# A list schedule that also picks the engine, and separate tiles for the first eight heads

## The chip, the cores and the metric

One Trainium2 chip, one of its cores. The metric is the device time of one execution in microseconds. The engines are named as in the profile: PE (TensorE, with its weight loads as PEld), DVE (VectorE), ACT (ScalarE), POOL (GpSimd), SP (SyncE, which here only issues DMAs). [...]

## What is computed

Attention whose queries and keys only meet when their hash buckets agree, for 4 batches of 8 heads (768 positions, head width 64), and behind it a feed-forward layer over 3072 tokens, 512 to 2048 to 512:

```python
q_bits = (np.einsum('bhsd,dk->bhsk', q, proj) > 0)      # six sign bits, k likewise
mask = q_bucket[:, :, :, None] == k_bucket[:, :, None, :]
scores = np.where(mask, scale * q @ k.T, -1e9)
attn = exp(scores - max) / (sum + 1e-9)
x = (attn @ v), heads side by side: 3072 x 512
g = s * relu(x @ w_in) ** 2 + b
out = g @ w_out
```

All inputs are 32-bit floats, except the two feed-forward weights, which arrive as 64-bit floats.

## The kernel before

**Work and staging.** The unit of attention work is a *slot*: 256 query rows of one head of one batch. There are 3 slots in a head, 24 in a batch, 96 in all. A *visit* is one head: its `prep` transposes queries and keys, splits both in a rounded high part and a remainder (`aq`, `bq`, `ks`), hashes them, and moves pieces between partitions with DMAs. `weights` makes the scores of a slot on PE (L436, L437), takes their negated maximum on DVE (L441), the exponential and its sum on ACT (L442), the inverse of the sum in four small DVE operations (L446 to L449), and scales the row on POOL (L454); the result is in one of four `eb` buffers. `values` transposes that on PE (L479), copies the transposed weights from PSUM to SBUF, and multiplies them with `v`.

For the first eight heads (`FULL = 8`, batch 0, slots 0 to 23) that product is made with plain 32-bit operands (L503; each appears as two matmuls in the profile), from copies that ACT makes for two of the three parts of a slot (L489) and DVE for the third (L487, `FD = (2,)`). For the other heads the copy is rounded on ACT (L494), the remainder is made on DVE (L495), and the product is four rounded matmuls (L510, L511). `values` ends with a copy of 64x256 to `xpb` (L526); every second head, both are split into `xsb` on ACT (L532) and DVE (L533) and sent to DRAM.

**Feed-forward.** `decode` loads one of 32 weight blocks (128x512 numbers of 64 bits) and makes a rounded part and a remainder of it: two ACT operations (L274, L275), two on DVE (L276, L277) and one on POOL (L278) join the two words of each number, then the rounded part is made on ACT (L280) and the remainder on POOL (L281). `moe` does one chunk of 256 tokens in eight steps, 96 steps in all: 24 matmuls of 256 columns (L569 to L571), three ACT operations (L575 to L577), two on POOL (L578, L579), and 12 matmuls of 512 columns (L590 to L592). A chunk can begin when it is through all eight heads of its batch, so the first comes behind slot 21.

**What sets the order.** Every operation is a step of `Plan` with an engine, a cost in microseconds that is written beside it, what it reads and writes, and a priority. `order` plays the engines forward with these costs and, on each, takes the ready step of the best priority; the result is each engine's instruction list, and on the chip each engine runs its list strictly in that order. Attention of slot `i` has priority around `10 * i`, decodes come a little behind, the feed-forward fills in where PE has nothing else. `decodes(i)` says how many of the 32 blocks may have been planned by slot `i`.

**Tiles that change type.** The buffers `PH` (the transposed weights) and `VS` (values) first hold plain 32-bit numbers for the first eight heads; `swap` later puts a tile of the rounded type in the same place.

## Time and profile before

| | |
|---|---|
| timed runs | 1095.40, 1088.42, 1095.47 us; median 1095.4 us |
| profiled execution | 1091.88 us, its span 1090.1 us |
| busy share of the span | PE 97%, PEld 86%, ACT 60%, DVE 56%, POOL 46% |
| instructions | 18596 |

How to read it: PE is the engine that is busy almost throughout, so the time is what PE works plus what it waits. A shown matmul lasts until its result is out, while the next one has begun long before; so waits shorter than that tail do not show as idle time, and the distance between two starts says more than the length. The program has four stretches: start-up (to 20 us), the 24 slots of batch 0 with next to no feed-forward to fill in (to 200 us), attention and feed-forward mixed (to about 880 us), and feed-forward alone.

### The profile page before, as it was taken

What the parts mean: (1) busy time and instruction counts of PE and PEld (TensorE: products, weight loads), DVE (VectorE), ACT (ScalarE), POOL (GpSimd) and SP (SyncE); (2) the same over time, 40 slices, a digit from 0 to 9 for tenths busy, and PEclk for the clock granted to TensorE, in tenths of its full rate; (3) what the DMA queues carried; (4) which work ended last, traced back from release to release, by engine and by line L of the source; (5) the groups of instructions that cost most, each with busy time, mean ns of one, the idle gap of its engine ahead of it and who ended that gap; (6) DMA issues with size and microseconds to landing.
All of it is one profiled execution on the core that took longest, in us unless ns stands there. A gap on an engine that the chain in (4) does not pass through costs nothing.

```text
span 1090.1 us, 18596 instructions
## 1 busy us (share of the span) xinstructions
PE 1062.0 (97%) x6948; PEld 942.4 (86%) x6948; DVE 612.9 (56%) x1181; ACT 654.4 (60%) x1265; POOL 502.1 (46%) x482
## 2 busy tenths in 40 slices
PE   7999888999999999999999999999999999999998
PEld 6666565898899999999999999999999998898987
DVE  5568886888666667666666766566667520000000
ACT  3567776888566666665666666656657553333332
POOL 2346776888644443444444443444444433333333
PEclk8999998999999999999999999999999999999999
DMA  3347565645322423332332243232323010101000
GB/s 80 83 134 201 160 189 141 160 118 175 80 55 62 121 74 82 94 92 65 92 104 64 74 112 84 54 115 66 83 54 118 3 56 33 58 1 59 17 23 20
DMA packets 85643, 94.14 MB, mean 86 GB/s; under 512 B 52832, under 2 KB 57952, under 8 KB 85552
## 3 DMA queue, kind: packets, MB, share of 16 engines
q1 hardware_dynamic: 80352, 75.90, 26.0%
q10 hardware_dynamic: 5200, 17.05, 5.1%
q8 instruction: 55, 0.90, 0.3%
q14 instruction: 36, 0.29, 0.1%
HBM read 48.24 MB, written 18.87 MB: 62 GB/s over the span
## 4 chain that ended last, share of the span: by engine, by line
PE 71%; issue 13%; POOL 8%; DVE 5%; ACT 2%; POOLq 0%; DVEq 0%; ACTq 0%
PE bank L479 11%; PE bank L436 6%; PE bank L437 6%; PE bank L503 5%; PE bank L569 5%; PE bank L570 5%; PE bank L571 5%; PE bank L590 5%; PE bank L511 5%; PE bank L591 5%; PE bank L592 5%; PE bank L510 4%; POOL glb L579 4%; POOL rb L578 3%; PE bank L318 2%
## 5 line engine op out<-in xcount | busy, mean ns | idle before, releaser
L454 POOL TENSOR_SCALAR eb<-eb,st 128x768 f32<-128x768 f32 x192 | 191.9, 1008 | 217.9 <-DVE st L449 175.2
L569 PE MATMUL bank<-xc,w 128*128 128x256 f32 x768 | 224.5, 292 | 0.0
L441 DVE TENSOR_REDUCE st<-bank 128x1 f32<-128x768 f32 x192 | 182.8, 954 | 73.9 <-PE bank L437 71.4
L570 PE MATMUL bank<-xc,w 128*128 128x256 f32 x768 | 217.0, 283 | 0.0
L571 PE MATMUL bank<-xc,w 128*128 128x256 f32 x768 | 216.9, 282 | 0.0
L442 ACT ACTIVATE eb<-bank,st 128x768 f32<-128x768 f32 x192 | 173.2, 903 | 43.3 <-DVE st L441 36.1
L494 ACT CAST phr<-bank 128x512 fp32r<-128x512 f32 x216 | 125.2, 583 | 123.1 <-PE bank L479 122.0
L578 POOL TENSOR_SCALAR rb<-rb,misc 128x512 f32<-128x512 f32 x96 | 74.8, 779 | 267.0 <-ACT ghb L577 255.7
L495 DVE TENSOR_TENSOR plb<-bank,phr 128x512 fp32r<-128x512 f32 x216 | 147.1, 686 | 80.2 <-ACT phr L494 77.9
L479 PE MATMUL bank<-ident,eb 128*128 128x128 f32 x1152 | 169.0, 276 | 4.4 <-POOL eb L454 2.9
L590 PE MATMUL bank<-w,ghb 128*128 128x512 f32 x384 | 156.5, 407 | 0.0
L592 PE MATMUL bank<-w,glb 128*128 128x512 f32 x384 | 151.4, 394 | 1.9 <-POOL glb L579 1.9
L591 PE MATMUL bank<-w,ghb 128*128 128x512 f32 x384 | 152.6, 398 | 0.0
L479 PEld LDWEIGHTS bank<-ident,eb 128*128 128x128 f32 x1152 | 135.8, 142 | 17.8 <-POOL eb L454 4.8
L569 PEld LDWEIGHTS bank<-xc,w 128*128 128x128 f32 x768 | 146.0, 190 | 4.3 <-issue 0.4
L570 PEld LDWEIGHTS bank<-xc,w 128*128 128x128 f32 x768 | 146.2, 190 | 3.1
L575 ACT ACTIVATE rb<-bank 128x512 f32<-128x512 f32 x96 | 57.5, 598 | 148.1 <-PE bank L571 145.7
L571 PEld LDWEIGHTS bank<-xc,w 128*128 128x128 f32 x768 | 146.0, 190 | 0.0
L436 PE MATMUL bank<-ks,aq 128*128 128x384 f32 x384 | 139.7, 364 | 3.6 <-ACT eb L442 3.5
L437 PE MATMUL bank<-ks,bq 76*128 76x384 f32 x384 | 131.9, 343 | 1.5 <-DVE bq L395 1.5
L579 POOL TENSOR_TENSOR glb<-rb,ghb 128x512 fp32r<-128x512 f32 x96 | 124.2, 1293 | 6.2
L510 PE MATMUL bank<-phr,vsr 128*128 128x256 f32 x432 | 115.1, 288 | 0.0
(88 smaller groups left out, 1723.3 us busy)
## 6 DMA issues: line engine op xcount, KB each, us to landing
xd<-xsb SPq DMA_DIRECT2D x48, 256.0 KB
xc<-xd SPq DMA_DIRECT2D x48, 256.0 KB
ks<-aq SPq DMA_DIRECT2D x30, 384.0 KB
raw<-in_moe_w_in_dram ACTq DMA_DIRECT2D x16, 512.0 KB
raw<-in_moe_w_out_dram ACTq DMA_DIRECT2D x16, 512.0 KB
nat<-in_q_dram SPq DMA_DIRECT2D x32, 192.0 KB
nat<-in_k_dram SPq DMA_DIRECT2D x32, 192.0 KB
ks<-bq SPq DMA_DIRECT2D x30, 192.0 KB
```

Source lines behind the costliest of these rows:

```text
L436: nc.tensor.matmul(o, aq[:, ts], ks[:, 0, cols], start=True, stop=False)
L437: nc.tensor.matmul(o, bq[0:HR, ts], ks[0:HR, 1, cols], start=False, stop=True)
L441: dve(S, lambda a=a, sc=sc: nc.vector.tensor_reduce(nm[:, a:a + 1], sc, AX.XY, ALU.max, negate=True), bk, [nk[a]], pr, 0.95)
L442: act(S, lambda a=a, sc=sc, e=e: nc.scalar.activation(e.rearrange("p (g n) -> p g n", g=2), sc, AF.Exp, bias=nm[:, a:a + 1], accum_out=z[: ...
L454: pool(S, lambda a=a, e=e: nc.gpsimd.tensor_scalar(e, e, rz[:, a:a + 1], u[:, a:a + 1], ALU.mult, ALU.add), [("st", y, 2)], [ek], pr, 1.01)
L479: nc.tensor.transpose(out=bank[:, tb, o:o + P], in_=eb[:, es[a], kt * P:(kt + 1) * P], identity=ident)
L569: nc.tensor.matmul(hp, w[:, 0, fs], xc[:, 0, :], start=(cc == 0), stop=False)
L570: nc.tensor.matmul(hp, w[:, 1, fs], xc[:, 0, :], start=False, stop=False)
L571: nc.tensor.matmul(hp, w[:, 0, fs], xc[:, 1, :], start=False, stop=(cc == NC_ - 1))
L590: nc.tensor.matmul(o, gh[:, ts], w[:, 0], start=(f == 0), stop=False)
L591: nc.tensor.matmul(o, gh[:, ts], w[:, 1], start=False, stop=False)
L592: nc.tensor.matmul(o, gl[:, ts], w[:, 0], start=False, stop=(f == NF - 1))
```

## The change

Five things change.

1. `Plan.any` takes a step with several *ways*, one for each engine that could do it. `order` lets the engine have it that would end it first by the written costs. Steps with two ways: the copies of transposed weights and of `xpb` (ACT or DVE), the relu (ACT or DVE), the output copies (DVE or ACT), the rounded part of `xsb` and of a decoded weight (ACT or POOL), and two copies of the first two visits (ACT or DVE). These copies all stand in the helper `copy`, L197 of the changed kernel.
2. The remainder of `xsb` moves from DVE to POOL.
3. `PH` and `VS` have the rounded type from the start. The plain values and weights of the first eight heads get tiles of their own, `VF` and `PF` (four of the latter instead of three), in the room of the last four weight blocks; `decode` of those four blocks waits until slot 23 is through with them.
4. The preparation of the first two visits works in halves of 384 columns, transposes queries and keys together (12 transposes instead of 24), and loads into the same layout as all others; the copy of `aq` to both halves of `ks` is two DMAs instead of one with a repeated source.
5. `decodes` starts two slots earlier and at a lower rate (`DSTART`, `FIRST`), four of the written costs change (among them 0.55 instead of 0.70 for the inverse), and the assumed DMA rate rises. `SMALL` and `SPLIT` are switches that keep the old way.

```diff
     def add(self, eng, cost, fn, r=(), w=(), pr=0.0, lag=0.0):
+        self.any([(eng, cost, fn)], r, w, pr, lag)
+
+    def any(self, ways, r=(), w=(), pr=0.0, lag=0.0):
...
+        def best(e, t):
+            found = None
+            for i in open_[e]:
+                if ready[i] > t + LOOK.get(e, 0.0):
+                    continue
+                ways, pr = self.steps[i][:2]
+                if found is not None and found[:2] <= (pr, i):
+                    continue
+                if len(ways) > 1:
+                    mine = max(t, ready[i]) + next(c for x, c, _ in ways if x == e)
+                    if any(max(free.get(x, 0.0), ready[i]) + c < mine - 1e-9 for x, c, _ in ways if x != e):
+                        continue
+                found = (pr, i)
+            return found
...
+    def some(n, fn, r, w, pr, ways):
+
+        cost = {ACT: 0.095 + n / 1050.0, DVE: (n + 64) / 960.0 + 0.05, POOL: 0.15 + n / 760.0}
+        eng = {ACT: nc.scalar, DVE: nc.vector, POOL: nc.gpsimd}
+        plan.any([(e, cost[e], lambda e=e: fn(eng[e])) for e in ways], r, w, pr)
...
-    VS = [wk.tile([P, 2, NT, D], F32, tag=f"vs{x}", name=f"vf{x}") for x in range(2)]
+    VS = [tile_(f"vs{x}", [P, NT, 2, D], F32R) for x in range(2)]
+    VF = [wk.tile([P, NT, D], F32, tag=f"w{ND_ - 1 - x}", name=f"vf{x}") for x in range(2)]
+    PF = [wk.tile([P, 2, 2 * CH], F32, tag=f"w{ND_ - 3 - x}", name=f"pf{x}") for x in range(2)]
+    PF = [z[:, y].rearrange("p (m q) -> p m q", m=2) for z in PF for y in range(2)]
...
-    PH = [wk.tile([P, 2, CH], F32, tag=f"ph{y}", name=f"pf{y}") for y in range(NPH)]
+    PH = [tile_(f"ph{y}", [P, 2, CH], F32R) for y in range(NPH)]
...
-        plan.add(None, 0.0, new, [], rk, pr - 5)
+        held = {ND - 1: [("vf", 0)], ND - 2: [("vf", 1)], ND - 3: [("pf", 0), ("pf", 1)], ND - 4: [("pf", 2), ("pf", 3)]}.get(u, [])
+        plan.add(None, 0.0, new, [], rk + held, pr - 5)
...
-        act(512, lambda: nc.scalar.copy(wt[key][:, 0], g), [gk], [key + (0,)], pr)
+        copy(512, lambda: wt[key][:, 0], lambda: g, [gk], [key + (0,)], pr, (ACT, POOL))
...
-                dma(lambda: ks[0:D], lambda: aq[D:P].rearrange("p (o n) -> p o n", o=1).broadcast_to([D, 2, S]), ...
+                for z in range(2):
+                    dma(lambda z=z: ks[z][0:D], lambda: aq[D:P], AK(x, r=(1,)), [("ks", x, 0, z)], pr, D * S * 4)
...
-        dve(1, inverse, nk + zk, [("st", y, 2)], pr, 0.70)
+            dve(1, inverse, nk + zk, [("st", y, 2), ("st", y, 3)], pr, 0.55)
...
-            if w < FULL:
-                if f in FD:
-                    dve(512, lambda: nc.vector.tensor_copy(ph(), src), [("b", tb)], [("ph", y)], pr, 0.65)
-                else:
-                    act(512, lambda: nc.scalar.copy(ph(), src), [("b", tb)], [("ph", y)], pr)
+            if full:
+                copy(512, lambda: ph, lambda: src, [("b", tb)], [("pf", y)], pr, (ACT, DVE))
                 return y
...
-            act(512, lambda: nc.scalar.copy(ph(), src), [("b", tb)], [("ph", y)], pr)
+            copy(512, lambda: ph, lambda: src, [("b", tb)], [("ph", y)], pr, (ACT, DVE))
...
-            act(CH, lambda: nc.scalar.copy(xsb[:, 0, :], t), xk, [("xs", 0)], pr)
-            dve(CH, lambda: nc.vector.tensor_tensor(xsb[:, 1, :], t, f32(xsb[:, 0, :]), ALU.subtract), ...
+            copy(CH, lambda: xsb[:, 0, :], lambda: t, xk, [("xs", 0)], pr, (ACT, POOL))
+            pool(CH, lambda: nc.gpsimd.tensor_tensor(xsb[:, 1, :], t, f32(xsb[:, 0, :]), ALU.subtract), ...
...
-        return min(ND, int(FIRST * max(0, i - EARLY // 3)) if i < EARLY else 8 + int(RATE * (i - EARLY)))
+        n = int(FIRST * max(0, i - DSTART)) if i < EARLY else int(FIRST * (EARLY - DSTART)) + int(RATE * (i - EARLY))
+        return min(n, ND if i >= H * NCH else ND - 4)
...
-FIRST = 1.2
+FIRST = 0.8
+DSTART = 5
-RATE_DMA = 1.9e5
+RATE_DMA = 2.2e5
```

Places in the instruction lists. `nat`, `aq`, `bq`, `ks` end in 69, 71 and the like for visit 0 (odd heads: 70, 72); `st` holds the maxima and sums, `pf` the transposed weights of the first eight heads, `eb` the exponentials. An `x2` is two instructions of that kind in a row.

DVE at start-up, before: the reductions of slot 0 (L441) come between the two visits' preparations.

```order
L393 TENSOR_SCALAR ks_71<-bank,misc 12x768
L395 TENSOR_SCALAR bq_69<-bank,misc 12x768
L367 TENSOR_TENSOR ks_72<-bank,ks_72 64x768
L441 TENSOR_REDUCE st<-bank 128x1 x2
L375 SCALAR_TENSOR_TENSOR bq_70<-bank,aq_68 64x768
L446 TENSOR_SCALAR st<-st 128x2
L447 TENSOR_SCALAR st<-st 128x2
L448 RECIPROCAL st<-st 128x2
L449 SCALAR_TENSOR_TENSOR st<-st 128x2
L393 TENSOR_SCALAR ks_72<-bank,misc 12x768
L395 TENSOR_SCALAR bq_70<-bank,misc 12x768
```

DVE at start-up, changed (L470 is the reduction):

```order
L427 TENSOR_SCALAR ks_71<-bank,misc 12x384
L429 TENSOR_SCALAR bq_69<-bank,misc 12x384
L406 SCALAR_TENSOR_TENSOR bq_70<-bank,aq_68 64x384
L408 TENSOR_TENSOR ks_72<-bank,ks_72 64x384
L406 SCALAR_TENSOR_TENSOR bq_70<-bank,aq_68 64x384
L408 TENSOR_TENSOR ks_72<-bank,ks_72 64x384
L427 TENSOR_SCALAR ks_72<-bank,misc 12x384
L429 TENSOR_SCALAR bq_70<-bank,misc 12x384
L427 TENSOR_SCALAR ks_72<-bank,misc 12x384
L429 TENSOR_SCALAR bq_70<-bank,misc 12x384
L470 TENSOR_REDUCE st<-bank 128x1 x3
```

All of the second visit's preparation now stands ahead of the first reduction.

DVE in slots 1 to 3, before: one copy of transposed weights (L487) in a slot.

```order
L441 TENSOR_REDUCE st<-bank 128x1 x2
L487 COPY pf_79<-bank 128x512
L441 TENSOR_REDUCE st<-bank 128x1
L446 TENSOR_SCALAR st<-st 128x2
L447 TENSOR_SCALAR st<-st 128x2
L448 RECIPROCAL st<-st 128x2
L449 SCALAR_TENSOR_TENSOR st<-st 128x2
L441 TENSOR_REDUCE st<-bank 128x1
```

The same place, changed (L197 is the copy that may stand on either engine, L487 to L490 the four small operations):

```order
L470 TENSOR_REDUCE st<-bank 128x1 x2
L487 TENSOR_SCALAR st<-st 128x2
L488 TENSOR_SCALAR st<-st 128x2
L489 RECIPROCAL st<-st 128x2
L490 SCALAR_TENSOR_TENSOR st<-st 128x2
L197 COPY pf_78<-bank 128x512
L470 TENSOR_REDUCE st<-bank 128x1
L197 COPY pf_78<-bank 128x512 x2
L487 TENSOR_SCALAR st<-st 128x2
```

DVE has up to two copies in a row here, and the small operations of the next slot stand behind them.

POOL around the first decode, before: scaling of rows (L454) and a decode's two operations (L278, L281), nothing else.

```order
L454 TENSOR_SCALAR eb<-eb,st 128x768 x14
L278 TENSOR_TENSOR osb<-osb,raw_192 128x512
L454 TENSOR_SCALAR eb<-eb,st 128x768 x2
L281 TENSOR_TENSOR w_644<-osb,w_644 128x512
L454 TENSOR_SCALAR eb<-eb,st 128x768 x2
```

POOL around the first decode, changed (L495 scales the rows, L320 and L323 are the decode's, L565 and the two kinds of L197 are new on this engine):

```order
L565 TENSOR_TENSOR xsb<-xpb,xsb 128x256
L495 TENSOR_SCALAR eb<-eb,st 128x768 x2
L320 TENSOR_TENSOR osb<-osb,raw_196 128x512
L197 CAST w_639<-osb 128x512
L197 CAST xsb<-xpb 128x256
L323 TENSOR_TENSOR w_639<-osb,w_639 128x512
L565 TENSOR_TENSOR xsb<-xpb,xsb 128x256
L495 TENSOR_SCALAR eb<-eb,st 128x768 x2
```

Between two scalings there are now up to five other operations.

## The prediction

> **What bounds the kernel now.** I read the page first (shares, slices), then the stretches of the span, then the groups of instructions inside the stretch where PE is not full, then single rows for the true distance of matmuls. The first two lines are PE's share and its forty slices.

> ```profile
> PE 1062.0 (97%) x6948; PEld 942.4 (86%) x6948; DVE 612.9 (56%) x1181; ACT 654.4 (60%) x1265; POOL 502.1 (46%) x482
> PE   7999888999999999999999999999999999999998
> ```

> PE is busy 97% of the span; its slices are under 9 at the start, in slices 4 to 6 and in the last. The stretches say where (columns: PE, weight loads, DVE, ACT, POOL busy, granted clock, DMA share, GB/s):

> ```profile
> 0.00:20.00 20.00, 13.52 (x69) 10.02 (x69) 11.04 (x39) 6.13 (x9) 4.79 (x11) 0.99 0.41 108
> 20.00:200.00 180.00, 167.28 (x887) 116.60 (x887) 134.31 (x253) 126.30 (x258) 102.42 (x90) 0.96 0.54 148
> 200.00:300.00 100.00, 98.35 (x676) 91.00 (x676) 80.05 (x131) 77.65 (x152) 77.14 (x67) 1.00 0.45 126
> 300.00:900.00 600.00, 598.29 (x4165) 560.33 (x4164) 380.44 (x748) 378.82 (x753) 251.02 (x252) 1.00 0.30 79
> 900.00:1080.00 180.00, 179.30 (x1139) 160.88 (x1138) 5.53 (x8) 63.95 (x94) 64.73 (x63) 1.00 0.08 28
> ```

> From 200 us to the end of the table PE idles 4.1 us in 880. What an engine other than PE saves there buys nothing. From 20 to 200 us, the 24 slots of batch 0, PE idles 12.7 us, and its matmuls are too few for the time: 887 in 180 us against 676 in 100 us. Its groups in that stretch, and rows with back-to-back starts:

> ```profile
> L503 PE MATMUL bank<-pf,vf 128*64 128x256 f32 x288 | 73.1, 391 | 5.6 <-ACT pf L489 3.9 <-DVE pf L487 1.5
> L479 PE MATMUL bank<-ident,eb 128*128 128x128 f32 x288 | 42.1, 287 | 3.7 <-POOL eb L454 2.9 <-DVE nat L336 0.8
> L436 PE MATMUL bank<-ks,aq 128*128 128x384 f32 x97 | 38.1, 393 | 2.2 <-ACT eb L442 2.0
> L318 PE MATMUL bank<-ident,nat 128*128 128x128 f32 x48 | 8.5, 287 | 0.0
> L331 PE MATMUL bank<-aq,pjh 128*64 128x384 f32 x15 | 5.8, 385 | 1.2 <-DVE bq L321 1.2
> ...
> 133.76 0.34 PE L436 MATMUL bank<-ks,aq 128*128 128x384 f32 x1
> 133.94 0.34 PE L437 MATMUL bank<-ks,bq 76*128 76x384 f32 x1
> 134.11 1.48 PE L479 MATMUL bank<-ident,eb 128*128 128x128 f32 x12
> 135.52 2.80 PE L503 MATMUL bank<-pf,vf 128*64 128x256 f32 x12
> ```

> Dense, a score matmul takes 0.175 us (133.76 to 134.11 for two), a transpose 0.118 (134.11 to 135.52 for twelve), an L503 at most 0.233 (2.80 for twelve). So the stretch holds 288 x 0.233 + (288 + 48) x 0.118 + 2 x 97 x 0.175 + 3 x 15 x 0.175 = 67 + 40 + 34 + 8 = 149 us of work, with the few feed-forward matmuls at its end about 151. Of the other 29 us some 7 are clock (next rows); some 22 are waits, of which the profile shows 12.7 as idle. These 22 us are what this change can reach.

> ```profile
> 12.00:19.00 7.00, 4.08 (x23) 2.77 (x22) 6.01 (x10) 3.36 (x6) 1.64 (x2) 1.00 0.25 56
> 19.00:26.00 7.00, 7.00 (x26) 5.80 (x26) 4.66 (x5) 2.53 (x6) 1.94 (x2) 0.53 0.00 0
> 165.00:173.00 8.00, 5.90 (x36) 4.50 (x36) 6.03 (x13) 5.75 (x14) 6.75 (x6) 1.00 0.80 201
> 173.00:180.00 7.00, 6.33 (x20) 4.39 (x20) 4.46 (x8) 4.08 (x8) 4.72 (x5) 0.51 0.61 150
> ```

> Twice a stretch in which PE idled two or three microseconds is followed by one of 7 us at half the clock, worth about 3.4 us each. [...] The timed runs lie at 1088.4 and 1095.4, the profiled one at 1091.9: steps of 3.5 us, so I read them (an estimate) as one, three and two such stretches.

> **The change, part by part.** The sum is against the profiled execution, 1091.9 us, 3.5 under the median of 1095.4. DVE, ACT and POOL in the same stretch, 20 to 200 us, with three rows of the whole run at the end (L418, L368, L603):

> ```profile
> L441 DVE TENSOR_REDUCE st<-bank 128x1 f32<-128x768 f32 x49 | 46.2, 952 | 20.8 <-PE bank L437 20.6
> L277 DVE SCALAR_TENSOR_TENSOR osb<-osb,raw 128x512 int32<-128x512 int32 x20 | 18.1, 909 | 0.3
> L487 DVE COPY pf<-bank 128x512 f32<-128x512 f32 x24 | 16.4, 685 | 7.0 <-PE bank L479 6.9
> L276 DVE TENSOR_SCALAR raw<-osb 128x512 int32<-128x512 int32 x20 | 12.3, 622 | 0.0
> L449 DVE SCALAR_TENSOR_TENSOR st<-st 128x2 f32<-128x2 f32 x24 | 9.6, 398 | 0.9
> L448 DVE RECIPROCAL st<-st 128x2 f32<-128x2 f32 x24 | 4.0, 166 | 0.0
> L533 DVE TENSOR_TENSOR xsb<-xpb,xsb 128x256 fp32r<-128x256 f32 x11 | 7.9, 715 | 0.6 <-ACT xsb L532 0.6
> ...
> L489 ACT COPY pf<-bank 128x512 f32<-128x512 f32 x48 | 27.2, 585 | 16.0 <-PE bank L479 15.7
> L280 ACT CAST w<-osb 128x512 fp32r<-128x512 f32 x19 | 11.8, 619 | 4.6 <-POOL osb L278 4.4
> ...
> L454 POOL TENSOR_SCALAR eb<-eb,st 128x768 f32<-128x768 f32 x50 | 52.4, 1056 | 53.8 <-DVE st L449 35.1 <-issue 7.1 <-PE bank L479 4.7
> L278 POOL TENSOR_TENSOR osb<-osb,raw 128x512 int32<-128x512 int32 x19 | 25.2, 1331 | 19.0 <-ACT eb L442 7.5 <-DVE st L446 4.4 <-DVE osb L277 4.4
> L281 POOL TENSOR_TENSOR w<-osb,w 128x512 fp32r<-128x512 f32 x19 | 24.5, 1293 | 5.5 <-ACT w L280 5.4
> ...
> L418 POOL TENSOR_TENSOR vsr<-vn,vsr 128x384 fp32r<-128x384 f32 x24 | 25.3, 1054 | 43.8 <-ACT vsr L417 43.6
> L368 POOL CAST ks<-ks 64x768 fp32r<-64x768 f32 x2 | 1.6, 821 | 4.0 <-ACT ks L366 3.9
> L603 DVE COPY osb<-bank 128x256 f32<-128x256 f32 x4 | 1.5, 420 | 42.4 <-PE bank L592 42.4
> ```

> *PE's own work.* The lists hold the same matmuls but for 12 transposes of the first two visits: 12 x 0.118 = **-1.4 us**.

> *Copies of the transposed weights, free engine and four buffers.* L503 shows 5.6 of the 12.7 us of idle, nearly all behind such a copy. In proportion that is 10 of the 22 us. Up to the 48th reduction the lists give DVE 39 of these copies instead of 23, and ACT 16 fewer, so a copy no longer waits behind an exponential for ACT. But a copy still takes 0.6 to 0.7 us and its product cannot come earlier. Between 0 and -10 I take half, **-5 us**.

> *DVE's load.* Up to the same reduction: 16 copies more (16 x 0.685 = 11.0), five decodes more (22 instead of 17 pairs of L276 and L277, 5 x 1.53 = 7.7), four copies of 64x256 more (at most 4 x 0.42 = 1.7), ten xsb remainders fewer (10 x 0.715 = -7.2): +13 us on 134. DVE waits 20.8 us before its reductions, for PE; so the 13 us find room, but copies now stand ahead of the small operations, on which POOL's scaling waits (35.1 us behind L449). Between 0 and +13 I take **+2**, near the room.

> *POOL's load.* Up to the 48th scaling: 14 weight casts and 5 xsb casts (L368, for as many elements a partition: 0.55 and 0.27), 11 remainders of 256 (L418, two thirds: 0.70), four decodes (2.62 each): 7.7 + 1.4 + 7.7 + 10.5 = +27 us on 102 of 180. The transposes wait 2.9 us for POOL now; by load that becomes 3.7, and with a scaling behind up to five other operations up to 8 more. I take **+1**. There is a second price: L449 means 398 ns here, where L448, its neighbour of the same size, takes 166, and L533 means 715. 24 x 0.23 = 5.6 us of such delay; if it goes with POOL's load, times 129/102, it costs DVE +1.5 us more, which is left inside DVE's term and stands in the rival below. [...]

> *ACT.* 16 copies fewer (-9.4) and 8 weight casts fewer (-5.0), four decodes more: its load falls. ACT bounds nothing here, so nothing beyond the copies' term.

> *Start-up.* Halves let a visit's chain overlap. But the second visit's preparation on DVE moves ahead of the first reduction:

> ```profile
> 14.80 0.96 DVE L441 TENSOR_REDUCE st<-bank 128x1 f32<-128x768 f32 x1
> 19.19 1.94 POOL L454 TENSOR_SCALAR eb<-eb,st 128x768 f32<-128x768 f32 x2 [1.69 <-DVE st L449]
> ```

> Eight half operations of 0.5 to 0.7 us now stand before that reduction, where one of 0.95 stood: slot 0's scaling comes some 2 us later than 19.2, slot 1's some 1 earlier, since nothing stands between any more. Cover: the scores of slot 1, which PE has in hand. **0**, between -3 and +3. The values of heads 8 and 9 are now loaded and cast at once: half a microsecond on ACT, in its idle start.

> *After 200 us.* 90 of 216 rounded copies go to DVE, ACT is relieved, POOL gets the remainders; DVE stays near 70%, and PE idled 4.1 us in 880. Decodes end two slots earlier although four blocks wait for slot 23. With a remainder following its copy on one engine the product may wait less: **-1**, between -3 and +3. The drain is unchanged. The second issue of each `ks` copy is 30 more DMAs on SP, whose transfers were a repeated source before: 0.

> Sum: -1.4 - 5 + 2 + 1 + 0 - 1 = -4.4, so **1087.5 us**, with the same two half-clock stretches; 0.7% under the median.

> **The rivals.** *Nothing in total*: PE's waits change their cause and not their sum; the shorter PE list alone gives 1090.5 (1086 to 1095). For it: waits in this stretch are spread over six causes, no one above 6 us. Against: the largest is the one that the change attacks.

> *DVE becomes the bound of batch 0* (slower). Its load there becomes 134 + 13 + 1.5 = 149 us. At today's ratio of load to time, 134/180, the stretch would need 200 us: +20. At least half of the 13 us lands if copies, which wait for PE in DVE's list, hold up reductions behind them: +8. This gives 1100 to 1112, 1107 in the middle. It decides from the point where DVE's 20.8 us of waiting before reductions is used up. For it: POOL and DVE both get fuller, and the written costs are too low: 0.55 us for the inverse, when L448 and L449 alone take 0.56. Against: that very wait.

> *The stretch closes up*: with buffers and engines free, waits fall by two thirds of 22 us (200 to 300 us shows that PE can run with 1.7 us of idle in 100 while the others are 80% busy), and with the waits one or both half-clock stretches go: -1.4 - 14.5 - 3.4 to -6.8, about 1071. Against: feed-forward work fills PE there, and batch 0 has none.

> **How the numbers follow.** Forecast 0.42, nothing 0.18, DVE 0.20, closing up 0.20. About 1% of 1095.4, 11 us, is what a measurement of this kernel tells from no change; so faster means under 1084.4, slower over 1106.4. The forecast's own range is 1081 to 1094, a half-clock stretch either way; a quarter of it is faster. Faster: 0.42 x 0.27 + 0.20 = 0.31. Slower: most of DVE's case, 0.16, and 0.01 for the rest. Same: 0.52. Range: half of the closing-up case below 1071 and half of DVE's above 1107 are left out.

> **What would show it.** Right: between 20 and 200 us fewer microseconds for the same 24 slots, idle before the L503 matmuls well under 5.6, idle before reductions down from 20.8 but not gone, POOL there near 130 us, the last three stretches as full as now. Wrong: idle before reductions under 5 us and PE idle above 15 (DVE bound); transposes waiting for scaling by more than 8 us (POOL); more or fewer than two half-clock stretches; or PE idle of more than 8 us after 200 us, which nothing here prices.

## The result and the profile after

The changed kernel takes 1100.6 us (median of 9 runs, 1099.3 to 1101.7) beside 1095.3 for the one before (9 runs, 1088.1 to 1095.8). The ratio is 1.0069, 95% interval 1.0048 to 1.0089: it is slower by 0.7%. (The quotient of the two medians is 1.0049: of the nine runs before, three lie at 1088 us and six at 1095 to 1096, and the median is one of the six. The quotient of the means is 1.0074.) That lies within the 1% that the prediction took for no change, and inside its whole range, 1071 to 1107, but above the range of the forecast itself, 1081 to 1094. The forecast was 0.7% faster: the sign is wrong. The profiled execution took 1100.8, its span is 1099.0 against 1090.1.

PE's totals and slices of the changed kernel, and the same stretches as before (columns: PE, weight loads, DVE, ACT, POOL busy, granted clock, DMA share, GB/s):

```profile
PE 1066.2 (97%) x6936; PEld 947.5 (86%) x6936; DVE 646.6 (59%) x1258; ACT 599.7 (55%) x1124; POOL 558.4 (51%) x562
PE   7989988899999999999999999999999999999998
```

```profile
20.00:200.00 180.00, 160.08 (x814) 110.57 (x815) 136.66 (x255) 107.49 (x214) 123.23 (x114) 0.93 0.51 148
300.00:900.00 600.00, 600.00 (x4196) 564.61 (x4196) 411.20 (x810) 347.41 (x668) 278.90 (x293) 1.00 0.30 79
900.00:1080.00 180.00, 180.00 (x1149) 163.44 (x1148) 0.00 (x0) 69.81 (x104) 65.29 (x64) 1.00 0.10 33
```

From 20 to 200 us PE does 814 matmuls where it did 887, at a clock of 0.93 where it was 0.96. From 300 us on it is even fuller than before (600.00 of 600 against 598.29). So the loss is early, and some is won back late. By the first transpose of a slot (the instruction that ends the wait for softmax) I split the 8.9 us of span:

| stretch | before | after | difference |
|---|---|---|---|
| start to slot 0 | 22.4 | 27.8 | +5.4 |
| slot 0 to slot 9 | 61.1 | 69.0 | +7.9 |
| slot 9 to slot 24 | 116.8 | 118.0 | +1.2 |
| slot 24 to the end | 889.8 | 884.2 | -5.6 |

**Start.** Single rows of the changed kernel's timeline, in order of time (start, duration, engine, line, operation):

```profile
8.47 0.56 DVE L408 TENSOR_TENSOR ks<-bank,ks 64x384 fp32r<-64x384 f32 x1
...
14.37 0.55 DVE L406 SCALAR_TENSOR_TENSOR bq<-bank,aq 64x384 fp32r<-64x384 f32 x1 [0.28 <-ACT ks L197]
...
17.65 0.67 DVE L427 TENSOR_SCALAR ks<-bank,misc 12x384 fp32r<-12x384 f32 x1 [1.00 <-PE bank L425]
...
20.42 1.82 DVE L470 TENSOR_REDUCE st<-bank 128x1 f32<-128x768 f32 x2
25.89 1.95 POOL L495 TENSOR_SCALAR eb<-eb,st 128x768 f32<-128x768 f32 x2 [5.79 <-DVE st L490]
```

The eight half operations of the second visit run from 14.37 to 20.42, waits of 0.28 and 1.00 us between them; the first reduction comes at 20.42 (before: 14.80) and the first scaling at 25.89 (before: 19.19).

**Slots 0 to 9.** PE's groups from 20 to 200 us, the last column the idle time before them and its cause:

```profile
L535 PE MATMUL bank<-pf,vf 128*64 128x256 f32 x265 | 69.0, 399 | 3.6 <-DVE pf L197 2.0 <-ACT pf L197 1.4 <-issue 0.2
L520 PE MATMUL bank<-ident,eb 128*128 128x128 f32 x272 | 42.3, 292 | 6.8 <-POOL eb L495 6.5
L465 PE MATMUL bank<-ks,aq 128*128 128x384 f32 x92 | 37.8, 410 | 10.4 <-ACT eb L471 10.3
```

Idle before the weighted values (L535, before: L503) went from 5.6 to 3.6, as meant; before the transposes it rose from 3.7 to 6.8, and before the scores (L465, before: L436) from 2.2 to 10.4, nearly all of that behind the exponential on ACT. The longest of these waits, from the chain of waits:

```profile
54.82 0.74 POOL xsb L565
55.58 7.58 DMA xd<-xsb
63.18 0.04 ACTq L197
63.26 0.40 ACT xsb L197
63.88 0.49 issue
64.61 0.69 PE bank L465
```

The transfer of the first split output takes 7.58 us. ACT's next instruction is the rounding of the next output into the same single buffer; it starts at 63.26 us, behind a wait of 4.63, and the exponential that follows it in ACT's list at 63.57. What ACT's and PE's rows say of it, with the loads' issue ahead:

```profile
55.18 1.49 ACTq L314 DMA_DIRECT2D raw<-in_moe_w_in_dram  x2
55.58 1.14 SPq L173 DMA_DIRECT2D xd<-xsb  x1
63.26 0.40 ACT L197 CAST xsb<-xpb 128x256 fp32r<-128x256 f32 x1 [4.63 <-DMA xd<-xsb]
63.57 0.89 ACT L471 ACTIVATE eb<-bank,st 128x768 f32<-128x768 f32 x1
64.61 0.69 PE L465 MATMUL bank<-ks,aq 128*128 128x384 f32 x1 [3.92 <-ACT eb L471]
```

Two weight loads of 512 KB were issued in the 0.4 us before the transfer (the `x2` row begins with the first; the second comes together with the transfer). PE idles 3.92 us, and the stretch after it runs at half the clock (third column from the end):

```profile
57.00:63.80 6.80, 3.69 (x23) 2.79 (x21) 3.02 (x4) 0.91 (x3) 1.24 (x3) 1.00 0.62 210
63.80:70.60 6.80, 6.00 (x18) 3.62 (x18) 3.31 (x7) 3.73 (x8) 4.25 (x5) 0.50 0.47 154
```

There are five such stretches before 200 us now, from 9.2 (6.8 us long), 19.4 (10.2), 63.8 (6.8), 87.7 (3.4) and 186.7 (6.8): 34 us at a clock of 0.50, which by an estimate from that clock cost up to 17 us, against two of 6.8 us before (0.50 too), up to 6.8. The difference, up to 10 us, is as large as the whole loss.

### The profile page after: what moved, and what is told of

Its sections match the earlier page's. It is cut to its first block, busy times and chain, and to the rows that moved or that the text cites. A ratio compares the mean times of both kernels' runs of the same rounds, so it can differ in the third digit from the quotient of the medians.

```text
span 1099.0 us, 18646 instructions
## 1 busy us (share of the span) xinstructions
PE 1066.2 (97%) x6936; PEld 947.5 (86%) x6936; DVE 646.6 (59%) x1258; ACT 599.7 (55%) x1124; POOL 558.4 (51%) x562
## 4 chain that ended last, share of the span: by engine, by line
PE 65%; issue 15%; POOL 9%; DVE 7%; ACT 1%; DMA 1%; POOLq 0%; DVEq 0%; ACTq 0%
PE bank L520 10%; PE bank L465 6%; PE bank L466 5%; PE bank L601 5%; PE bank L602 5%; PE bank L603 5%; POOL glb L611 5%; PE bank L543 5%; PE bank L624 5%; PE bank L542 4%; PE bank L622 4%; PE bank L623 4%; PE bank L535 3%; POOL rb L610 3%; DVE st L470 2%
## 5 line engine op out<-in xcount | busy, mean ns | idle before, releaser
L495 POOL TENSOR_SCALAR eb<-eb,st 128x768 f32<-128x768 f32 x192 | 197.7, 1037 | 200.2 <-DVE st L490 163.9
L603 PE MATMUL bank<-xc,w 128*128 128x256 f32 x768 | 216.9, 282 | 0.0
L470 DVE TENSOR_REDUCE st<-bank 128x1 f32<-128x768 f32 x192 | 181.9, 954 | 58.2 <-PE bank L466 51.7
L471 ACT ACTIVATE eb<-bank,st 128x768 f32<-128x768 f32 x192 | 172.8, 901 | 63.8 <-DVE st L470 61.7
L527 DVE TENSOR_TENSOR plb<-bank,ph 128x512 fp32r<-128x512 f32 x216 | 145.0, 685 | 27.0 <-ACT ph L197 25.0
L520 PEld LDWEIGHTS bank<-ident,eb 128*128 128x128 f32 x1152 | 136.3, 142 | 25.0 <-POOL eb L495 12.5
L465 PE MATMUL bank<-ks,aq 128*128 128x384 f32 x384 | 141.7, 369 | 10.9 <-ACT eb L471 10.9
L603 PEld LDWEIGHTS bank<-xc,w 128*128 128x128 f32 x768 | 146.3, 191 | 0.0
L607 ACT ACTIVATE rb<-bank 128x512 f32<-128x512 f32 x88 | 52.6, 597 | 168.8 <-PE bank L603 161.8
L611 POOL TENSOR_TENSOR glb<-rb,ghb 128x512 fp32r<-128x512 f32 x96 | 124.1, 1293 | 5.8
L197 ACT CAST ph<-bank 128x512 fp32r<-128x512 f32 x126 | 73.3, 585 | 95.2 <-PE bank L520 91.3
```

The source lines that it names most:

```text
L465: nc.tensor.matmul(o, aq[:, ts], ks[0][:, cols], start=True, stop=False)
L470: dve(S, lambda a=a, sc=sc: nc.vector.tensor_reduce(nm[:, a:a + 1], sc, AX.XY, ALU.max, negate=True), bk, [nk[a]], pr, 0.95)
L495: pool(S, lambda a=a, e=e: nc.gpsimd.tensor_scalar(e, e, rz[:, a:a + 1], u[:, a:a + 1], ALU.mult, ALU.add), [("st", y, 2), ("st", y, 3)], ...
L520: nc.tensor.transpose(out=bank[:, tb, o:o + P], in_=eb[:, es[a], kt * P:(kt + 1) * P], identity=ident)
L603: nc.tensor.matmul(hp, w[:, 0, fs], xc[:, 1, :], start=False, stop=(cc == NC_ - 1))
L611: pool(2 * CH, lambda r=r, gh=gh, gl=gl: nc.gpsimd.tensor_tensor(gl, r, f32(gh), ALU.subtract), [rk, hk], [lk], MP)
```

## The experiments

Three suspects come out of that: the order of the start, the new rule for how many weights are decoded by each slot (the loads), and the single buffer of the split outputs, which the loads make late. The choice of engines is the fourth. Each edit makes the scheduler draw up every list anew, so its ratio holds whatever that moves besides. Ratios go to runs of the kernel before on the same chip in the same set; since its median differed between the sets (1094.4, 1091.3, 1095.7, 1093.1 for four experiments each, in order), I compare ratios.

**e1, the start alone.** All of the first visit's preparation first, then the second's.

```diff
-            p_(0, -90 + 5 * w)
+            p_(0, -90 + 85 * w)
```

> The changed kernel, with the second visit's preparation at a lower priority than slot 0, so that DVE has the first two reductions ahead of most of it. Theory A (the order at start-up costs some 5 us that are never won back): the first scaling moves from 25.9 us to about 21, the first transposes of weights from 27.8 to about 23, and the time falls by 4 to 6 us, to 1095 to 1097. Theory B (start-up is slow because PE runs at half clock there, whatever the order on DVE): the first transposes come at most 2 us earlier and the time stays within 2 us of 1100.6. Theory C (DVE and POOL are too full in batch 0): start-up is not the place, the time stays within 2 us as well.

Measured: 1096.5 us (10 runs), ratio 1.0034 (1.0014 to 1.0055). First reduction at 15.45, slot 0 at 21.5, as theory A had it. The start's order costs about 4 us; the 4.1 us wait of ACT for the output's transfer is still there.

**e2, two buffers for the split outputs of batch 0**, in the space of a weight block that is decoded later.

```diff
+    XF = wk.tile([P, 2, 2, CH], F32R, tag=f"w{ND_ - 5}", name="xf")
...
-            copy(CH, lambda: xsb[:, 0, :], lambda: t, xk, [("xs", 0)], pr, (ACT, POOL))
+            xs, sk = (XF[:, len(xd) % 2], ("xf", len(xd) % 2)) if bb == 0 else (xsb, ("xs",))
+            copy(CH, lambda: xs[:, 0, :], lambda: t, xk, [sk + (0,)], pr, (ACT, POOL))
...
```

> The changed kernel, with two buffers instead of one for the split attention outputs of batch 0 (in the room of one more late weight block), so that the rounding on ACT no longer waits for the transfer of the one before. Theory D (one late transfer holds ACT for 4.6 us at 58 to 63 us, PE stands still 3.9 us and then runs at half clock for 7): the stall and the half-clock stretch at 63 to 70 us go, slot 9's transposes come at about 89 us instead of 96.8, and the time falls by 5 to 8 us, to 1093 to 1096. Rival (the pace there is set by load on DVE and POOL): the waits turn up under another name, slot 9 stays later than 94 us and the time stays within 2 us of 1100.6.

Measured: 1098.1 (10 runs), ratio 1.0037 (1.0011 to 1.0063). The wait is gone and slot 6 comes at 65.6 instead of 71.7, but slot 9 at 92.2, 4.6 sooner, and the end only 2.5: other half-clock stretches now stand at 81, 129 and 262 us (the clock from 20 to 200 us is 0.94). Neither theory D (1093 to 1096) nor its rival (at least 1098.6) gives this time: the stall was real, and worth less than it looked.

**e3, the old rule for the decodes alone.**

```diff
-        n = int(FIRST * max(0, i - DSTART)) if i < EARLY else int(FIRST * (EARLY - DSTART)) + int(RATE * (i - EARLY))
+        n = int(FIRST * max(0, i - EARLY // 3)) if i < EARLY else 8 + int(RATE * (i - EARLY))
...
-FIRST = 0.8
+FIRST = 1.2
```

> The changed kernel with the old rule for how many weight blocks may be decoded by a slot (first at slot 8, 1.2 a slot), so one weight load instead of two stands ahead of the first output transfers. Theory D (the transfer is late because two loads of 512 KB stand before it): the stall at 58 to 63 us is halved or gone, the time falls by 3 to 7 us. Theory C (load of DVE and POOL in batch 0): fewer decodes early help too, but evenly over the slots and without a single stall vanishing, by 2 to 4 us. If neither holds, the time stays within 2 us of 1100.6.

Measured: 1093.5 (10 runs), ratio 0.9996 (0.9977 to 1.0014): 7 us, the largest of the four. The start's two half-clock stretches are the only ones left before the last microseconds (clock 0.83 up to 20 us, 0.97 from 20 to 200). The stall did not vanish: with one weight load ahead of it the transfer still takes 5.85 us, and ACT waits 2.89 for it where it waited 4.63.

**e4, the choice of engines taken back.** Each two-way step gets the engine that it had before (but for the two copies of the first two visits, which keep the choice), and the remainder of the split output goes back to DVE. One of its lines:

```diff
...
-                copy(512, lambda: ph, lambda: src, [("b", tb)], [("pf", y)], pr, (ACT, DVE))
+                copy(512, lambda: ph, lambda: src, [("b", tb)], [("pf", y)], pr, (DVE,) if f == 2 else (ACT,))
...
```

> The changed kernel with each two-way step held to the engine that the kernel before uses, the remainder of the split outputs back on DVE too; tiles, start-up and decodes stay as changed. If the choice of engines is what loads DVE and POOL in batch 0 (theory C), batch 0 ends some 8 to 12 us earlier than the changed kernel's 214 us and the time falls to 1092 to 1096. If the loss is start-up order and one late transfer (theories A and D), batch 0 still ends later than 208 us, the small gain after 230 us (21 us of excess spacing on PE instead of 33) is lost, and the time rises to 1103 to 1108.

Measured: 1099.4 (10 runs), ratio 1.0054 (1.0032 to 1.0077), the same as with the choice and in neither of the two ranges expected: slot 24 comes 6 us sooner (208.8), and what was won after it is lost again.

**e5, e1 and e3 together.**

> The changed kernel with both single edits that gave time back: DVE has the first reductions ahead of the second visit's preparation, and weight blocks are decoded by the old rule. If the two losses are separate (4.2 and 7.2 us by the runs so far), the time is 1088 to 1091, the first transposes come near 21.5 us and slot 24's near 199, no later than in the kernel before. If they are the same loss seen twice (half-clock stretches that one of the edits happens to shift), the time stays at 1092 to 1095.

Measured: 1090.9 (10 runs), ratio 0.9982 (0.9965 to 0.9999). Without its two costs the change is 0.2% faster than before. ACT still waits 4.9 us for the output's transfer.

**e6, e1, e2 and e3 together.**

> As the run with both edits, and two buffers for the split outputs of batch 0. If the old decode rule has already taken the transfer out of ACT's way (theory D), the buffers add nothing: within 2 us of that run. If other transfers still hold ACT, 2 to 5 us less.

Measured: 1082.7 (4 runs), ratio 0.9925 (0.9897 to 0.9953): faster than both kernels, and 8 us less than e5, where the expectation gave the second buffer 5 at most. Between the start and the last microseconds of the span no stretch is at half clock (clock 0.76 up to 20 us, 0.99 from 20 to 200).

**e7, e5 with e4's fixed engines.**

> As the run with both edits, but each two-way step held to the engine of the kernel before and the remainder of the split outputs on DVE. The difference to that run is what the choice of engines is worth by itself. If it gives the denser PE after batch 0 (6 to 12 us less excess spacing there) and costs nothing in batch 0, this run is 4 to 8 us slower than the run with both edits; if the choice overfills DVE and POOL in batch 0, it is 2 to 5 us faster.

Measured: 1089.2 (10 runs), ratio 0.9971 (0.9953 to 0.9989), inside e5's interval: 1.7 us less, which is in neither range expected, and no worth of the choice that stands out from chance.

**e8, the kernel before with the new rule alone.**

```diff
-    return min(ND, int(FIRST * max(0, i - EARLY // 3)) if i < EARLY else 8 + int(RATE * (i - EARLY)))
+    return min(ND, int(FIRST * max(0, i - 5)) if i < EARLY else int(FIRST * (EARLY - 5)) + int(RATE * (i - EARLY)))
```

(with FIRST at 0.8)

> The kernel before with one thing changed: weight blocks are decoded by the new rule (from slot 6 on at 0.8 a slot). If the new rule costs time by itself, because two loads then stand before the outputs' transfers, this is 4 to 8 us slower than the kernel before. If it only costs where ACT's list has the rounding of the next output right behind the loads, as in the changed kernel, it is within 2 us of the kernel before.

Measured: 1097.0 (10 runs), ratio 1.0038 (1.0015 to 1.0060). The rule costs the old kernel 4 us too.

**e9, e10, e11, e12: all three edits less one each, and all three again.** e9 keeps the new rule (e1 and e2), e10 keeps the new start (e2 and e3), e11 has all three and e4's fixed engines, e12 is e6 once more.

> The changed kernel with the first visit's preparation first and with two buffers for the split outputs, and the new rule for the decodes kept. Theory A (the earlier decodes cost time only because their loads hold up the output transfers, and two buffers end that): the same as with the old rule, 1081 to 1086. Theory B (the earlier decodes cost what they cost whatever the buffers are, since their operations stand among those of batch 0): the two edits' own gains add up, 1100.6 - 4.2 - 2.5 = 1094, in any case over 1090. In the trace no rounding waits for a transfer under either.

> The changed kernel with the old rule for the decodes and two buffers for the split outputs; the second visit's preparation still ahead of the first reduction. If the three costs add up, the start-up order is worth its 4 us here too: about 1087 beside the 1082.7 of all three edits. If a quiet start only moves the half-clock stretches about, 1082 to 1085; if the start-up order was what let the other two edits work, over 1090.

> All three edits, and the two-way steps held to the engines that they had before the change. If the choice of engines is worth nothing in total: 1081 to 1085, as with the choice. If it pays once no transfer blocks an engine: 1086 to 1092, with rounded copies later and PE idle after 220 us. If it overfills POOL and DVE in batch 0: 1076 to 1081.

> The kernel with all three edits once more, beside the three that lack one of them. The same 1082.7 within 2 us, and a ratio to the kernel before of 0.988 to 0.996. If the first measurement was a lucky one, 1086 to 1091.

Measured: e9 1093.4 (ratio 0.9986, 0.9973 to 0.9999), e10 1088.0 (0.9931, 0.9908 to 0.9954), e11 1086.6 (0.9920, 0.9903 to 0.9938), e12 1084.2 (0.9900, 0.9884 to 0.9916). e12 repeats e6, and e10 lies near the 1087 of costs that add up. With the changed kernel and e1, e2, e3, e5 this makes all eight combinations of three edits; each edit, taken alone on top of the four combinations of the others, in per cent of the time before (two ratios of this precision differ by chance by up to 0.3; all three edits together are taken from e12, and with e6, the same kernel in another set, the last column would be -0.06, -0.61 and -0.57):

| edit | on none | on one | on the other | on both |
|---|---|---|---|---|
| first visit first | -0.35 | -0.51 (buffers) | -0.14 (rule) | -0.31 |
| old rule | -0.73 | -0.52 (start) | -1.06 (buffers) | -0.86 |
| two output buffers | -0.32 | -0.48 (start) | -0.65 (rule) | -0.82 |

Each has the same sign in all four. For the old rule and the two buffers every value is beyond chance; for the start one or two of the four are not. e9 decides against its theory A: with two buffers no transfer is waited for, and the new rule still costs 9 us.

The engines of e11 (fixed) and then of e12 (chosen), two of PE's groups each from 20 to 200 us, show what the choice wins and what it loses:

```profile
L536 PE MATMUL bank<-pf,vf 128*64 128x256 f32 x288 | 73.1, 388 | 5.6 <-ACT pf L197 4.4 <-DVE pf L197 1.2
L521 PE MATMUL bank<-ident,eb 128*128 128x128 f32 x292 | 42.5, 282 | 2.1 <-POOL eb L496 1.9 <-DVE bq L364 0.2
```

```profile
L536 PE MATMUL bank<-pf,vf 128*64 128x256 f32 x288 | 74.8, 397 | 2.5 <-ACT pf L197 1.6 <-DVE pf L197 0.8
L521 PE MATMUL bank<-ident,eb 128*128 128x128 f32 x292 | 43.7, 280 | 6.2 <-POOL eb L496 5.9 <-DVE bq L364 0.2
```

PE waits 3.1 us less for the copies and 4.1 us more for POOL's scaling, which now has POOL's new casts and remainders ahead of it. In total no pair differs beyond chance: fixed is 0.15 and 0.11% faster (e4, e7) and 0.20% slower (e11, whose 1086.6 is at the edge of "it pays"; 0.05% faster beside e6). The three pairs agree on where the choice gains and loses (start of slot 24, and from there to the end of the span):

| engines | chosen | fixed |
|---|---|---|
| after and e4 | 214.8 + 884.2 | 208.8 + 889.9 |
| e5 and e7 | 202.9 + 886.5 | 196.3 + 890.3 |
| e12 and e11 | 198.3 + 885.2 | 195.5 + 889.8 |

It loses 3 to 7 us up to slot 24 and wins 4 to 6 after it.

**What the new rule costs without the transfer's wait: e13 to e16.** In e9 ACT's first operation of a decode waits 12.5 us (ten times, between 20 and 210 us) for POOL to free one of the two decode buffers, in e12 5.0 us (seven times). e13 is e9 with four such buffers, e14 is e12 with four.

```diff
+    OF = wk.tile([P, 2, DM], F32, tag=f"w{ND_ - 6}", name="of")
...
-        g, gk = osb[:, u % 2, :], ("os", u % 2)
+        o4 = u % 4 if u < ND - 6 else u % 2
+        g, gk = (osb if o4 < 2 else OF)[:, o4 % 2, :], ("os", o4)
...
```

> The kernel with the new rule, the start-up order and two buffers for the split outputs, and now four buffers in place of two for the weights under decoding. Theory C (the new rule costs time because ACT, in order, waits for POOL to free a decode buffer): 1085 to 1088, and ACT's wait for POOL before a decode under 3 us (12.5 with two). Theory D (the load itself, on POOL and DVE, in slots 7 to 24): 1091 to 1095, the wait gone all the same.

> All three edits and four decode buffers. Under theory C, 1 to 3 us less than with two (1084.2), since 5.0 us of the same wait stand there too; under D the same within 1 us.

Measured: e13 1103.1 (4 runs), ratio 1.0094 (1.0070 to 1.0117); e14 1092.1 (10 runs), 0.9987 (0.9974 to 0.9999). The wait is gone in both, and both are slower, by 1.1% and 0.9%, which neither theory foresaw. The scarce buffer was a brake more than a cost: without it the schedule draws still more decodes into batch 0 (27 ended by slot 24 where e9 has 21, and 25 where e12 has 20). Both runs also hold back one more block, but that is not the cost: from slot 24 to the end they need 883.1 and 883.7 us, less than e9's 889.6 and e12's 885.2. In e13 POOL is busy 80 of these 89 us, PE 73:

```profile
103.00:192.00 89.00, 73.49 (x369) 50.16 (x366) 73.73 (x127) 59.81 (x119) 79.93 (x68) 0.92 0.59 168
```

e15 is e9 with only the first part of the rule (up to slot 20) new, e16 with only the second.

```diff
-        n = int(FIRST * max(0, i - DSTART)) if i < EARLY else int(FIRST * (EARLY - DSTART)) + int(RATE * (i - EARLY))
+        n = int(FIRST * max(0, i - DSTART)) if i < EARLY else 8 + int(RATE * (i - EARLY))                   # e15
+        n = int(1.2 * max(0, i - EARLY // 3)) if i < EARLY else 12 + int(RATE * (i - EARLY))               # e16
```

> The start-up order, two output buffers, and of the new rule only its first part: the first decodes one slot earlier, and fewer by slots 14 to 20 (12 by slot 20 in place of 15), then the old count. If the earlier first loads cost the 9 us: 1090 to 1094. If the second part does, four decodes more in slots 22 to 24: 1083 to 1087.

> The counterpart: the old count up to slot 20, and then four decodes more by each slot from 22 on, as in the new rule. The complement of the run before: 1083 to 1087 if the first part costs the time, 1090 to 1094 if the second does; both about 1088 if each takes half.

Measured: e15 1088.8 (10 runs), 0.9967 (0.9950 to 0.9983); e16 1081.8 (4 runs), 0.9899 (0.9875 to 0.9924). By the ratios the first part costs 0.7% beside e16 of the same set, the second nothing (e16 beside e12's 0.9900); the times themselves lie 1 us under the ranges expected. In its first part the rule allows one decode more than the old one at slots 7 to 10 (so the first comes one slot earlier, not two), and fewer from 12 to 20. It is not POOL's load over the stretch: between 20 and 200 us POOL is busy 130.49 us in e9 and 130.49 in e12. Part of the loss shows in slots 6 to 9, first of e9, then of e16:

```profile
61.80:86.70 24.90, 22.06 (x116) 14.65 (x115) 19.83 (x38) 16.79 (x34) 20.48 (x18) 1.00 0.58 170
```

```profile
61.80:83.20 21.40, 21.07 (x114) 14.16 (x112) 17.68 (x33) 13.43 (x27) 15.04 (x15) 1.00 0.61 176
```

The same three slots take 24.9 us and 21.4. PE has the same work but idles 2.8 us instead of 0.3, and POOL, DVE and ACT carry more. Single rows of e9 there, then the first two pairs of scalings of e16:

```profile
67.14 3.15 POOL L496 TENSOR_SCALAR eb<-eb,st 128x768 f32<-128x768 f32 x2 [0.63 <-DVE st L491]
67.44 0.68 DVE L320 SCALAR_TENSOR_TENSOR osb<-osb,raw 128x512 int32<-128x512 int32 x1
...
73.91 0.68 DVE L320 SCALAR_TENSOR_TENSOR osb<-osb,raw 128x512 int32<-128x512 int32 x1
74.17 2.92 POOL L496 TENSOR_SCALAR eb<-eb,st 128x768 f32<-128x768 f32 x2 [0.60 <-DVE st L491]
74.97 1.27 DVE L320 SCALAR_TENSOR_TENSOR osb<-osb,raw 128x512 int32<-128x512 int32 x1
77.06 2.55 POOL L321 TENSOR_TENSOR osb<-osb,raw 128x512 int32<-128x512 int32 x2
77.15 1.42 PE L521 MATMUL bank<-ident,eb 128*128 128x128 f32 x11 [1.06 <-POOL eb L496]
79.57 2.52 POOL L324 TENSOR_TENSOR w<-osb,w 128x512 fp32r<-128x512 f32 x2
84.84 1.95 POOL L496 TENSOR_SCALAR eb<-eb,st 128x768 f32<-128x768 f32 x2 [2.75 <-DVE st L491]
```

```profile
67.69 2.12 POOL L496 TENSOR_SCALAR eb<-eb,st 128x768 f32<-128x768 f32 x2 [1.45 <-DVE st L491]
74.41 1.95 POOL L496 TENSOR_SCALAR eb<-eb,st 128x768 f32<-128x768 f32 x2 [0.62 <-DVE st L491]
```

Two pairs of scalings take 3.15 and 2.92 us where e16's take 2.12 and 1.95: beside them DVE runs the two-input operation of an early decode (L320), and PE stands still for 1.06 us behind the second pair. The two decodes that POOL then does stand between two pairs of scalings, but they are not what the next pair waits for: POOL is free 2.75 us before DVE releases it (84.84). By the number of decodes that POOL has ended at slot 9's first transpose, the time from slot 6 to slot 9 falls into groups:

| decodes by slot 9 | kernels | slots 6 to 9, us |
|---|---|---|
| 1 | e7, e11 | 19.9, 20.5 |
| 2 | before, e3, e5, e6, e10, e12, e14, e16 | 20.6 to 22.5 |
| 2, two more begun | e4 | 23.3 |
| 3 | e8 | 24.2 |
| 4 | after, e1, e2, e9, e13, e15 | 25.0 to 26.6 |

An early decode goes with some 2 us there. Slots 6 to 9 are a third of the whole: e9's profiled execution is 10.8 us longer than e16's, 3.6 of it in slots 6 to 9, 2.6 in slots 9 to 24 and 4.7 behind them, where a stall at 253 us (PE waits 0.96 and 1.05 us) is followed by one more half-clock stretch (the clock from 200 to 300 us is 0.98, in e16 1.00). Nor is the time won back by having more blocks ready: with 27 decodes ended by slot 24, e13 needs 883.1 us from there to the end, e12 with 20 needs 885.2, but slot 24 comes at 216.6 and 198.3.

## Why the prediction went wrong

*PE's bound: right.* The loss is in the part that was named as the only one with slack, and after 300 us PE has none.

*PE's own work, -1.4: right* in count (6948 to 6936 matmuls), too small to be seen by itself.

*Copies, -5: right in kind, smaller in size.* PE's visible idle before L535 fell by 2.0 (5.6 to 3.6), by 3.1 in e12 beside e11.

*POOL's load, +1 (0 to +8): mis-sized.* Idle before the transposes rose by 3.1 in the changed kernel and by 4.1 from e11 to e12. The term's load was counted rightly (129 us; 123 in the changed kernel, 130 in e12), but not what it does to the scalings that stand behind it in line; the two terms together are -4 in the sum and about zero in the three pairs. Up to slot 24 the choice of engines even loses (3 to 7 us): what the rival "nothing in total" said, that PE's waits change their cause and not their sum, is nearest to it.

*Start-up, 0 (-3 to +3): wrong.* The step "slot 0's scaling comes some 2 us later" measured 6.7: the eight operations were seen, but set off against what they displaced, and their own waits (0.28 and 1.00) and the clock (0.50 from 19.4 to 29.6 us) were not counted. Cover by slot 1's scores failed: PE ran out of work, slot 0's transposes came 5.4 us late, and about 4 of that stays in the total (e1).

*The decodes: the step that failed most.* The five more decodes by slot 24 were counted as load on DVE and POOL, spread over 180 us, and the rule itself was set at no cost beyond it. What counts is where they stand: four instead of two before slot 9 go with 2.6 us more in slots 6 to 9 (25.1 against 22.5); and an output's transfer that began just behind two weight loads took 7.58 us (3.6 before, behind one load 2.9 us ahead) and held up ACT's list for 4.63. I had named no queue behind that wait, because before shows none: there ACT never waits for the output's buffer. Taking the rule back is worth 0.5 to 1.1% in the four pairs, 6 to 12 us. Little of that is the transfer's wait: the old rule leaves one load of the two, and in e9 and e12, where no transfer is waited for, the rule's cost is 0.9% as well. The text said of the decodes' earlier end only that four blocks wait for slot 23.

*"With the same two half-clock stretches": wrong.* Five stretches, and up to 10 us. The text had named this as what would show it wrong. By an estimate from the clock of 0.50, a stall that such a stretch follows (the windows at the end show which) costs up to 1.7 us more for each 3.4 us of half clock, 1.7 to 5 us here, and a sum of stalls without that is short by so much.

*DVE as the bound: rightly the lesser case.* Idle before the reductions is still 19.8 us (20.8 before), where that rival needed it to be used up, and in e12, which is faster than both kernels, it is lower (14.4). The time came out on that rival's side by another mechanism.

*After 200 us, -1 (-3 to +3): too small.* From slot 24 to the end 5.6 us were won, and by the three pairs above 4 to 6 of them are the choice of engines. Behind the remainders of the rounded copies (L543, 220 to 1080 us) PE idles 1.1 us with the choice and 2.5 without it; the rest shows as no idle time, and where it comes from is not shown. That was the place where the forecast held that nothing could be bought.

```profile
L470 DVE TENSOR_REDUCE st<-bank 128x1 f32<-128x768 f32 x47 | 43.4, 951 | 19.8 <-PE bank L466 19.5
L490 DVE SCALAR_TENSOR_TENSOR st<-st 128x2 f32<-128x2 f32 x23 | 8.3, 360 | 0.8
L495 POOL TENSOR_SCALAR eb<-eb,st 128x768 f32<-128x768 f32 x46 | 52.8, 1158 | 37.2 <-DVE st L490 35.1 <-ACT pf L197 1.8 <-ACT raw L317 0.2
```

These rows of the changed kernel (20 to 200 us) also answer the +1.5 us of DVE's term, a delay that was to go with POOL's load. That was an estimate of mine, and no run shows it: the small operation L490 takes 360 ns where it took 398, not more, although POOL was fuller (123 against 102 us), while POOL's scaling rose from 1056 to 1158. In e9 and e12, with POOL busy 130 us of the same 180 in both, the small operation takes 257 and 316. What the runs showed in its place is a delay where the two engines' operations overlap, on POOL's side too, which the sum left out. DVE's two-input decode operation (20 to 200 us of all 18 traces) takes 670 to 703 ns, 100 times, when POOL is idle or starts later, and 1136 on average, 290 times, when POOL's operation was running already. A scaling takes 1348 ns on average with such an operation beside it (332 times) and 995 without one (537 times). The stretched pairs of e9 above are among them.

What stays open: how much of the early decodes' cost is their own delay and how much the half clock that follows. e9 has three more stretches of 3.4 us than e12 (mean clock 0.989 and 0.993), which by the clock of 0.50 is up to 5 of its 9 us; the two were not taken apart. No run moves the weight loads alone; that they make the transfer slow rests on the first transfer of all 18 traces (last section).

## What to carry to other kernels

A change that a scheduler spreads over four engines has to be costed by what stands in line ahead of the critical operation, and what runs beside it, at each place, not by load over a stretch: e9 and e12 have POOL equally busy in batch 0, 72% of the time, and lie 9 us apart. Undo the parts one at a time and in all combinations before judging the main idea: here the choice of engines had no worth that stands out from chance, and a start order and a count of early decodes, worth 3 to 4 and 8 to 9 us on the mean of four pairs, decided the sign; a second buffer that neither kernel had was worth about 6. Before you remove a wait by adding buffers, ask whether it is the brake that keeps background work out of the way.

## What the runs showed of the hardware

```profile
84.30:87.70 3.40, 1.82 (x12) 1.06 (x11) 2.37 (x4) 1.38 (x3) 3.40 (x3) 1.00 0.81 249
183.30:186.70 3.40, 1.74 (x10) 1.16 (x9) 3.37 (x8) 1.43 (x4) 2.14 (x2) 0.99 0.98 310
```

```profile
119.70:123.10 3.40, 1.73 (x12) 1.19 (x10) 3.25 (x5) 0.89 (x3) 3.40 (x3) 1.00 0.46 155
252.90:256.30 3.40, 1.39 (x10) 0.99 (x9) 3.37 (x8) 1.23 (x2) 1.80 (x3) 0.99 0.30 114
```

PE was busy about half of each (1.39 to 1.82 us), with no single gap above 1.5 us in the third. I cut all 18 traces, from the start-up's end to 1060 us, into such windows at full clock: 38 have PE busy for 1.97 us or less, and half clock follows 27 of them; it follows none of the more than 5300 others. So the count to make in these traces is of windows of 3.4 us in which PE works 1.97 us or less, not of idle gaps: each of the four above is half idle, and half clock follows.

*A transfer beside weight loads.* The first output transfer of a kernel (256 KB) is read back as soon as it has landed (in the changed kernel the transfer lasts from 55.58 to 63.16 us and the read-back is issued at 63.17), so the distance of these two issues on SP is its time. The rows of the kernel before, then of e5:

```profile
51.45 1.00 SPq L145 DMA_DIRECT2D xd<-xsb  x1
55.05 0.34 SPq L555 DMA_DIRECT2D xc<-xd  x1
...
54.30 1.14 SPq L173 DMA_DIRECT2D xd<-xsb  x1
60.90 0.33 SPq L587 DMA_DIRECT2D xc<-xd  x1
```

Over all 18 traces it goes with the weight loads of 512 KB that ACT has issued just ahead:

| weight loads ahead of the transfer | kernels | its time, us |
|---|---|---|
| none within 10 us | e4 | 2.7 |
| one, 2.9 us ahead | before | 3.6 |
| two, 2.2 and 2.6 us ahead | e8 | 5.0 |
| one, 0.2 to 0.4 us ahead | e3, e5, e6, e7, e10, e11, e12, e14, e16 | 5.6 to 6.7 |
| two, the first 0.4 us ahead | after, e1, e2, e9, e13, e15 | 6.7 to 8.0 |

With one load just ahead the transfer took 5.6 to 6.7 us where it took 2.7 with none; with a second load, 6.7 to 8.0. Two loads of queries and keys (192 KB each) also stand 0.7 to 2.3 us ahead on the transfer's own queue, except in e7 and e11; these two take 6.3 and 6.5, so those loads are not what makes it long.
